# A gated pair of spectral filters: the order of every engine's work set by a list scheduler at build time

## The chip, the core and the metric

The kernel runs on one NeuronCore of a Trainium2 chip. Time is device time in microseconds (us) of one execution. The core has a matrix engine (PE), a vector engine (DVE), an activation engine (ACT), a general engine (POOL) and a sync engine (SP) that issues most DMAs. Each engine runs its own queue strictly in program order, and waits on semaphores that other engines or DMAs raise. An instruction that waits holds up everything behind it on its engine. PE writes only to PSUM, from where ACT or DVE copies ("evicts") to SBUF.

## The reference

x is one 2048 x 1024 matrix in bf16. Two branches filter it in the frequency domain with their own complex weights, and a gate per row mixes them:

```
g = sigmoid((A_x * gate_w).sum(-1, keepdims=True))          # one value per row
a = irfft2(rfft2(A_x) * (A_w_r + 1j * A_w_i))               # 2048 x 513 weights each
b = irfft2(rfft2(A_x) * (B_w_r + 1j * B_w_i))
out = g * a + (1 - g) * b
```

Both branches transform the same x, so the forward transform is computed once; B_x is not read.

## The kernel before, in words

The two-dimensional transforms are matmuls with constant cosine and sine matrices, in stages of 16 tiles each. Every tile is 128 partitions x 1024 f32 in PSUM. There are three PSUM slots for tiles, and one spare bank for small results (`m7`).

- **Fold** (`fold`, L365): DVE folds x along D by sums and differences, two tiles per step in four instructions.
- **S1** (in the loop at L385): PE, first part of the transform along S; ACT evicts to `Z`.
- **Gate**: `gate_w` is folded by DVE on one partition (four 1x512 instructions), PE turns it into columns (`G8`), four *gate rows* (`gate_row`, L379; eight 1x512 matmuls, each needs four `Z` tiles) give the gate's spectrum, sixteen small matmuls and one DVE product (`ZG`) give the *gated matrix's* input.
- **D** (`stage_d`, L421) needs all 16 `Z` tiles, gives `Q`; **S2** (`stage_s2`, L434) gives `X`, the spectrum.
- **Product** (`prod(b, m)`, L452): DVE multiplies two `X` tiles with the weights of branch b, eight steps per branch, two 2048-wide and two 1024-wide instructions each. `p512` does the same for the edge column.
- **I1** (`stage_i1(b, kg)`, L469): PE, inverse along S, gives `V` of branch b. A small DMA (`v512_row`, L514) adds row 0 once all 16 `V` tiles are out.
- **Inverse D** (`stage_dinv(b, n2)`, L518) needs all of `V` and row 0, gives `VA` or `VB`.
- **Gate broadcast** (`gmix`, L559): PE, a sigmoid on ACT, then two DVE instructions scale the last transform's matrix by g and 1 - g.
- **Last stage** (`s1inv`, L587): PE adds both gated branches in PSUM, ACT or DVE evicts, DVE *unfolds* in four instructions, SP stores 256 KB per tile.

Weights are loaded by `wload(b)` (L340) in 18 DMAs of 16 partitions on SP's queue, behind x and the constants. A product of branch b waits for the whole of its branch's weights (key `("W", b)`).

The order on every engine is the order in which the code records operations (`Sched.op`); `solve` then works out the semaphore waits. That order is written out by hand: loops over t interleave D of tile t, S2 of t - 1, I1 of t - 5 and a product on every second t (L537), then I1 of B with inverse D of A three tiles later (L571), then inverse D of B one tile ahead of the last stage (L611). Slots go round in turn. `ev` (L296) gives an eviction to ACT or DVE, whichever has less work summed up so far.

Of the kernel before, what the change touches and what calls it, by code (L numbers as in the profile page):

```python
# [4 lines left out]
dt = mybir.dt  # L5
# [111 lines left out]
class Op:  # L117
    __slots__ = ("eng", "idx", "fns", "deps", "raw", "dma", "clock", "need", "count", "waits", "pos")
# [8 lines left out]
class Sched:  # L127
# [9 lines left out]
    def op(self, eng, fns, reads=(), writes=(), dma=False):  # L137
        if not isinstance(fns, (list, tuple)):
            fns = [fns]
        o = Op(eng, len(self.q[eng]), list(fns), dma, len(self.all))  # L140
# [14 lines left out]
        o.deps.discard(o)  # L155
        return o
# [78 lines left out]
def bass_gated_mix__spectral_gfnet__spectral_gfnet__prompt_kernel(  # L235
# [45 lines left out]


    load = {"act": 0.0, "dve": 0.0}
    slot_n = [0]
    nslots = [3]

    def slot():
        s = slot_n[0] % nslots[0]
        slot_n[0] += 1
        return s  # L290

    def dve(ns, fns, reads, writes):
        load["dve"] += ns
        return S.op("dve", fns, reads, writes)

    def ev(n, outap, inap, reads, writes, eng=None, bias=0.0):  # L296
        ca, cd = 170 + 0.833 * n, 150 + 1.04 * n
        if eng is None:
            eng = "act" if load["act"] + ca <= load["dve"] + cd + bias else "dve"
        load[eng] += ca if eng == "act" else cd  # L300
        if eng == "act":
            S.op("act", lambda e: e.activation(outap, inap, ACT.Copy), reads, writes)  # L302
        else:
            S.op("dve", lambda e: e.tensor_copy(outap, inap), reads, writes)  # L304
# [4 lines left out]
    def misc(b, off, dims, np_=128):  # L309
        return ap(PS, b * 512 + off, dims, 0, np_)  # L310

    def mm(o, l, r, start, stop):
        return lambda e: e.matmul(o, l, r, start=start, stop=stop, skip_group_check=True)  # L313

    def tt(o, a, b, op):
        return lambda e: e.tensor_tensor(out=o, in0=a, in1=b, op=op)  # L316

    def dma(eng, pairs, reads, writes, kind=True):
        S.op(eng, [lambda e, d=d, s=s: e.dma_start(d, s) for d, s in pairs], reads, writes, dma=kind)  # L319

    def cload(eng, t, key, n):
        dma(eng, [(ap(t, 0, [[1, n]]).bitcast(dt.uint16), cst[key].ap())], [], [key])


    def xload(a, b):
        dma("sp", [(ap(R1, a * 1024, [[1024, b - a], [1, 1024]]), xv[:, a:b, :])], [], [("x", i) for i in range(a, b)])

    xload(0, 2)
    cload("sp", FM, "F", 2048)
    dma("act", [(ap(R2, 2048, [[1, 1024]], 0, 1), gate_w.rearrange("(o d) -> o d", o=1))], [], ["gw"])  # L330
    cload("act", ONE, "ONE", 2)
    for a, b in ((2, 4), (4, 8), (8, 12), (12, 16)):
        xload(a, b)
    cload("sp", DM, "DM", 2048)
    cload("sp", S2, "S2", 768)
    cload("sp", KI, "KI", 1024)
    cload("sp", GS, "GS", 16)
    cload("sp", ID, "ID", 16)

    def wload(b):  # L340
# [4 lines left out]
        for pm in range(2):  # L345
            for ii in range(4):
                for c in range(2):
                    src = wsrc[b][c]
                    n = src.shape[-1]

                    def part(r0, step, k0, k1):
                        prs.append((AP(T, (4 * pm + ii) * P + (2 * k0 + c) * NS, [[8 * P, 16], [2 * NS, k1 - k0], [1, n]]),
                                    AP(src.tensor, src.offset + r0 * n, [[128 * n, 16], [step * n, k1 - k0], [1, n]])))
                    if pm == 0:
                        part(16 * ii, 1, 0, 16)
                    elif ii < 3:
                        part(80 + 16 * ii, -1, 0, 16)
                    else:
                        part(127, -1, 1, 16)
                        part(64, 1, 0, 1)  # L360
        dma("sp", prs, [], [("W", b)] + (["zrow", "gwt"] if b else []))
    wload(0)


    def fold(n, src, soff, tmp, st, dst, doff, p0, np_, ns, reads, skey, writes):  # L365
# [5 lines left out]
        dve(ns, tt(Sx, lo, hi, ALU.add), reads, [skey + ("S",)])  # L371
        dve(ns, tt(Tx, lo, hi, ALU.subtract), reads, [skey + ("T",)])
        f = ap(tmp, st, [[1024, n], [512, 2], [1, 256]], p0, np_)
        r = ap(tmp, st + 511, [[1024, n], [512, 2], [-1, 256]], p0, np_)
        for i, op in enumerate((ALU.add, ALU.subtract)):
            o = ap(dst, doff + 512 * i, [[1024, n], [256, 2], [1, 256]], p0, np_)
            dve(ns, tt(o, f, r, op), [skey + ("S",), skey + ("T",)], [w + (i,) for w in writes])

    def gate_row(c):  # L379
        fns = [mm(misc(6, 0, [[1, 512]], 1), ap(G8, q, [[1, 1]]), ap(R3, q * 2048 + c * 32, [[128, 16], [1, 32]]), q == 0, q == 7)  # L380
               for q in range(8)]
        S.op("pe", fns, ["G8"] + [("Z", 4 * c + i) for i in range(4)], ["m6"])
        ev(512, ap(R2, c * 512, [[8, 16], [128, 4], [1, 8]], 0, 1), misc(6, 0, [[32, 16], [8, 4], [1, 8]], 1), ["m6"], [("zrow", c)])

    for n2 in range(0, 16, 2):  # L385
        st = n2 // 2 % 2
        fold(2, R1, n2 * 1024, RING, st * 2048, R4, n2 * 1024, 0, 128, 680,
             [("x", n2), ("x", n2 + 1)], ("st", st), [("u", n2), ("u", n2 + 1)])
        for m in (n2, n2 + 1):
            s = slot()  # L390
            fns = []
            for q in range(8):
                fns.append(mm(pslot(s, q * 128, [[1, 128]]), ap(R4, m * 1024 + q * 128, [[1, 128]]),
                              ap(FM, m * 128, [[1, 128]]), True, True))
            S.op("pe", fns, [("u", m, 0), ("u", m, 1), "F"], [("ps", s)])
            ev(1024, ap(R3, m * 8, [[128, 128], [1, 8]]), pslot(s, 0, [[8, 128], [1, 8]]), [("ps", s)], [("Z", m)],
               eng="act")
        if n2 == 2:
            fold(1, R2, 2048, R2, 4096, R2, 3072, 0, 1, 380, ["gw"], ("gst",), [("ug",)])
            fns = [mm(misc(7, q, [[1, 1]]), ap(R2, 3072 + q * 128, [[1, 128]], 0, 1), ap(ONE, 0, [[1, 1]], 0, 1), True, True)  # L400
                   for q in range(8)]
            S.op("pe", fns, [("ug", 0), ("ug", 1), "ONE"], ["m7", "gwt"])
            ev(8, ap(G8, 0, [[1, 8]]), misc(7, 0, [[1, 8]]), ["m7"], ["G8"], eng="act")
        if n2 % 4 == 2 and n2 > 2:
            gate_row(n2 // 4 - 1)
    gate_row(3)
    NZ = 16
    fns = []
    for n2 in range(16):
        w = ap(R2, n2 * 128, [[1, 128]], 0, 1)  # L410
        fns.append(mm(misc(7, n2, [[1, 1]]), w, ap(ONE, 0, [[1, 1]], 0, 1), True, True))
    S.op("pe", fns, [("zrow", c) for c in range(4)] + ["ONE"], ["m7", "zrow"])
# [233 lines left out]
```

## Time and profile before

| | us |
|---|---|
| median of 3 runs (161.98 to 162.6) | 162.08 |
| the profiled execution's own time | 160.53 |
| its span, first to last instruction | 159.0 |
| busy: PE / DVE / ACT / POOL | 124.6 / 120.4 / 121.7 / 0.2 |
| mean granted TensorE clock | 0.968 |
| DMA, all queues | 19.53 MB |

In the profile's rows all matmuls have one line (L313), all DVE arithmetic L316, all copies L302 (ACT) or L304 (DVE), since helpers record them; so they are told apart by tile names and shapes. `R` stands for the big buffers R1 to R5. A row of the timeline has start, length, engine, line, operation, output<-input, count, and in brackets the engine's idle time before it with what ended it. A row of issues has a DMA's count, size and the time from issue to landing. SPq is SP's queue.

### The profile page before, as it was taken

What the parts mean: (1) busy time and instruction counts of PE and PEld (TensorE: products, weight loads), DVE (VectorE), ACT (ScalarE), POOL (GpSimd) and SP (SyncE); (2) the same over time, 40 slices, a digit from 0 to 9 for tenths busy, and PEclk for the clock granted to TensorE, in tenths of its full rate; (3) what the DMA queues carried; (4) which work ended last, traced back from release to release, by engine and by line L of the source; (5) the groups of instructions that cost most, each with busy time, mean ns of one, the idle gap of its engine ahead of it and who ended that gap; (6) DMA issues with size and microseconds to landing.
All of it is one profiled execution on the core that took longest, in us unless ns stands there. A gap on an engine that the chain in (4) does not pass through costs nothing.

```text
span 159.0 us, 2541 instructions
## 1 busy us (share of the span) xinstructions
PE 124.6 (78%) x1015; PEld 90.0 (57%) x1024; DVE 120.4 (76%) x193; ACT 121.7 (77%) x132; POOL 0.2 (0%) x4
## 2 busy tenths in 40 slices
PE   0255897888928999999954999959999899898930
PEld 0244654355616767776633788847778576565600
DVE  0699998000079997998999999969923788989892
ACT  3045889629985988989955599999999499888850
POOL 0000000000000000000000000000000000000000
PEclk9999999999999999999995599999999999999995
DMA  5899999999999999950000000000000034243333
GB/s 168 296 429 415 257 168 167 177 167 165 179 168 170 181 169 169 197 191 4 0 0 0 0 5 0 0 0 4 0 0 1 4 112 152 86 180 123 145 132 132
DMA packets 13165, 19.53 MB, mean 123 GB/s; under 512 B 1505, under 2 KB 9825, under 8 KB 12770
## 3 DMA queue, kind: packets, MB, share of 16 engines
q1 hardware_dynamic: 13008, 19.37, 53.5%
q8 instruction: 8, 0.13, 0.4%
q14 instruction: 3, 0.02, 0.1%
q10 hardware_dynamic: 146, 0.00, 0.0%
HBM read 15.17 MB, written 4.19 MB: 122 GB/s over the span
## 4 chain that ended last, share of the span: by engine, by line
ACT 37%; PE 27%; DVE 22%; issue 7%; DMA 4%; SPq 1%; DVEq 0%
PE PS L313 27%; ACT R L302 21%; ACT RING L302 13%; DVE RING L316 12%; DVE R L316 6%; DMA R<-in_A_x_dram 4%; DVE RING L304 4%; ACT GROW L564 1%; ACT L564 1%; ACT V L302 1%; SPq L319 1%; DVEq L213 0%
## 5 line engine op out<-in xcount | busy, mean ns | idle before, releaser
L302 ACT ACTIVATE R<-PS 128x1024 bf16<-128x1024 f32 (+1 forms) x80 | 75.9, 1041 | 20.9 <-PE PS L313 20.9
L316 DVE TENSOR_TENSOR RING<-R 128x2048 bf16<-128x2048 bf16 (+1 forms) x48 | 48.0, 1041 | 16.9 <-DMA R<-in_A_w_i_dram 10.2
L302 ACT ACTIVATE RING<-PS 128x1024 bf16<-128x1024 f32 x40 | 42.8, 1135 | 8.0 <-PE PS L313 6.8
L316 DVE TENSOR_TENSOR RING<-RING 128x512 bf16<-128x512 bf16 (+1 forms) x96 | 44.6, 509 | 2.5 <-ACT RING L302 1.4
L313 PE MATMUL PS<-KI,RING 128*128 128x256 bf16 x256 | 34.0, 281 | 7.5 <-issue 3.1
L313 PE MATMUL PS<-DI,R 128*128 128x256 bf16 x256 | 32.7, 273 | 1.5 <-DVE RING L304 1.2
L313 PEld LDWEIGHTS PS<-KI,RING 128*128 128x128 bf16 x256 | 24.3, 101 | 14.0 <-issue 3.9
L313 PEld LDWEIGHTS PS<-DI,R 128*128 128x128 bf16 x256 | 24.4, 98 | 8.4 <-DVE RING L304 2.2
L313 PE MATMUL PS<-FM,R 128*128 128x128 bf16 x128 | 11.8, 266 | 13.0 <-DVE R L316 13.0
L313 PEld LDWEIGHTS PS<-FM,R 128*128 128x128 bf16 x128 | 10.1, 122 | 14.8 <-DVE R L316 14.4
L313 PE MATMUL PS<-RING,S 128*128 128x1 bf16 (+2 forms) x91 | 15.8, 304 | 1.3 <-ACT RING L302 1.1
L313 PE MATMUL PS<-DM,R 128*128 128x256 bf16 x128 | 16.4, 273 | 0.2 <-DVE RING L304 0.2
L313 PEld LDWEIGHTS PS<-DM,R 128*128 128x128 bf16 x128 | 12.0, 98 | 2.5 <-DVE RING L304 0.5
L313 PEld LDWEIGHTS PS<-RING,S 128*128 128x128 bf16 x96 | 7.8, 97 | 7.7 <-ACT RING L302 1.4
L304 DVE CAST RING<-PS 128x1024 bf16<-128x1024 f32 x8 | 10.0, 1251 | 1.9 <-PE PS L313 1.9
L316 DVE TENSOR_TENSOR R<-RING 128x1024 bf16<-128x1024 bf16 x16 | 10.3, 688 | 0.3
L313 PE MATMUL PS<-R,FM 128*128 128x512 bf16 x30 | 9.1, 379 | 1.3 <-DVE RING L304 1.3
L313 PE MATMUL PS<-RING,DM 128*128 128x512 bf16 x30 | 9.1, 379 | 0.1
L313 PE MATMUL PS<-R,G 128*1 128x512 bf16 x32 | 7.5, 378 | 0.7 <-ACT R L302 0.7
L304 DVE CAST R<-PS 128x1024 bf16<-128x1024 f32 x4 | 4.9, 1223 | 3.1 <-PE PS L313 3.1
L316 DVE TENSOR_TENSOR ZG<-PS,GS 128x16 bf16<-128x16 f32 x1 | 0.2, 175 | 6.8 <-PE PS L313 6.8
L313 PEld LDWEIGHTS PS<-RING,DM 128*128 128x128 bf16 x32 | 3.1, 98 | 3.8
(25 smaller groups left out, 26.9 us busy)
## 6 DMA issues: line engine op xcount, KB each, us to landing
out_dram<-RING SPq DMA_DIRECT2D x16, 256.0 KB, 2.0
R<-in_A_x_dram SPq DMA_DIRECT2D x3, 1024.0 KB, 10.5
R<-in_A_w_r_dram SPq DMA_DIRECT2D x7, 256.5 KB, 13.9
R<-in_A_w_i_dram SPq DMA_DIRECT2D x7, 256.5 KB, 14.7
R<-in_B_w_r_dram SPq DMA_DIRECT2D x7, 256.5 KB, 14.4
R<-in_B_w_i_dram SPq DMA_DIRECT2D x7, 256.5 KB, 14.1
R<-in_A_x_dram SPq DMA_DIRECT2D x2, 512.0 KB, 5.0
FM<-c_F SPq DMA_DIRECT2D x1, 512.0 KB, 5.0
```

The costliest lines, as they stand in the source:

```text
L302: S.op("act", lambda e: e.activation(outap, inap, ACT.Copy), reads, writes)
L304: S.op("dve", lambda e: e.tensor_copy(outap, inap), reads, writes)
L313: return lambda e: e.matmul(o, l, r, start=start, stop=stop, skip_group_check=True)
L316: return lambda e: e.tensor_tensor(out=o, in0=a, in1=b, op=op)
L319: S.op(eng, [lambda e, d=d, s=s: e.dma_start(d, s) for d, s in pairs], reads, writes, dma=kind)
L564: S.op("act", lambda e: e.activation(ap(GROW, 0, [[1, 512]]), misc(7, 0, [[1, 512]]), ACT.Sigmoid), ["m7"], ["GROW"])
```

## The change

Operations are no longer recorded in the order of the code. Each becomes a unit `U` with its engine, what it reads and writes, units that must come before it, a priority, and a rough duration. `run` takes streams of units (one list per stage, in order within the list). At each step it computes when the head of every stream could start, from `Sched.ready`, and records the one of highest priority among those within 40 ns of the earliest. So a fixed order comes out at build time, different on each engine. An eviction becomes a unit when its tile is recorded, and goes to the engine that would finish it first; it frees its PSUM slot, and a new tile takes any free slot. Besides:

- The fold of `gate_w` goes from DVE to POOL.
- The last gate row waits for the spectrum's edge column (`x5`), so it and what follows from it (gated matrix, `ZG`) come after S2. The gate's spectrum lies in `RM`'s first partition, so the load of `RM` now waits for it.
- Weights A are loaded in two halves (18 and 16 DMAs of half the rows), and a product waits only for its half. Weights B stay whole.
- The first product of B writes to a third buffer (`FM`, free by then) and needs no place among A's two.

```
+    def ready(self, eng, reads, writes):
+        t = self.free[eng]
+        for k in list(reads) + list(writes):
+            for d in self.writer.get(k, ()):
+                t = max(t, d.end + (60 if d.eng == eng else 160))
+        for k in writes:
+            for d in self.readers.get(k, ()):
+                t = max(t, d.end + (0 if d.eng == eng else 160))
+        return t
...
+            if self.eng == "ev":
+                n = self.n
+                ca, cd = 200 + 0.833 * n, 180 + 1.04 * n
+                ta, td = S.ready("act", self.reads, w), S.ready("dve", self.reads, w)
+                return (ta, "act", ca) if ta + ca <= td + cd + (300 if dnext[0] < td + 400 else 0) else (td, "dve", cd)
...
+            t0 = min(c[0][0] for c in cand)
+            r, u, s = min((c for c in cand if c[0][0] <= t0 + 40), key=lambda c: (c[1].prio, c[0][0]))
+            s.remove(u)
+            u.emit(r)
...
-        dma("sp", prs, [], [("W", b)] + (["zrow", "gwt"] if b else []))
-    wload(0)
+        return U(("ldw", b, ka), "sp", prs, [], [("W", b, k) for k in range(ka, kb)] + (["gwt"] if b else []),
+                 after, dma=(True, 1500.0 * (kb - ka)))
...
+             cload("sp", GS, "GS", 16), cload("sp", ID, "ID", 16), wload(0, 0, 8), wload(0, 8, 16),
+             wload(1, 0, 16, after=["G8mm"]), cload("sp", DI, "DI", 2048),
+             cload("sp", RM, "RM", 2048, ["zrow"], after=["gspec"])]
...
-            fold(1, R2, 2048, R2, 4096, R2, 3072, 0, 1, 380, ["gw"], ("gst",), [("ug",)])
+    gfold = [fold("gfold", 1, R2, 2048, R2, 4096, R2, 3072, 0, 1, ["gw"], ("gst",), [("ug",)], eng="pool", after=[("ld", "gw")])]
...
-    gate_row(3)
+        return U(("grow", c), "pe", ops, ["G8"] + [("Z", 4 * c + i) for i in range(4)], ["m7"], prio=6,
+                 after=["G8"] + [("evZ", 4 * c + i) for i in range(4)] + (["x5"] if c == 3 else []),
...
-        r = [("X", 2 * m), ("X", 2 * m + 1), ("W", b)]
+        rd = [("X", 2 * m), ("X", 2 * m + 1), ("W", b, 2 * m), ("W", b, 2 * m + 1)]
+        ok = (2,) if (b, m) == (1, 0) else (0, 1)
...
+        return U(("prod", b, m), "dve", ops, rd, after=[("evX", 2 * m), ("evX", 2 * m + 1), ("ldw", b, 0)], can=can, prio=2 + b)
...
-    for t in range(16 + 5):
-        if t < 16:
-            stage_d(t)
-        if 1 <= t < 17:
-            stage_s2(t - 1)
-        if t >= 5:
-            stage_i1(0, t - 5)
-        if t >= 2 and t % 2 == 0:
-            prod(t // 18, t // 2 - 1 - t // 18 * 8)
...
+    run([loads, aloads, folds, gfold, gate, [s1(n) for n in R16], [stage_d(k) for k in R16], [stage_s2(k) for k in R16],
+         [prod(0, m) for m in range(8)], [prod(1, m) for m in range(8)], [stage_i1(0, k) for k in R16],
+         [stage_i1(1, k) for k in R16], x5, [p512(0), p512(1)], [v512(0), v512(1)],
+         [stage_dinv(0, n) for n in R16] + [stage_dinv(1, n) for n in R16], [gmix(c) for c in range(4)],
+         [s1inv(n) for n in R16]])
```

Three places show what came of it. First PE, at the end of S1: `FM,R` are S1 tiles (eight matmuls each), `R,G` gate rows, `ONE,R` the gate's small matmuls, `DM,R` D tiles, `RING,S` S2. Before:

```order
L313 MATMUL PS<-FM,R 128x128 x32
L313 MATMUL PS<-R,G 1x512 x16
L313 MATMUL PS<-ONE,R 128x1 x16
L313 MATMUL PS<-DM,R 128x256 x16
L313 MATMUL PS<-RING,S 128x512 x2
```

Now:

```order
L314 MATMUL PS<-FM,R 128x128 x32
L314 MATMUL PS<-R,G 1x512 x8
L314 MATMUL PS<-FM,R 128x128 x16
L314 MATMUL PS<-DM,R 128x256 x24
L314 MATMUL PS<-RING,S 128x512 x2
```

Gate row 2 now stands ahead of the last two S1 tiles, gate row 3 and the gate's sixteen matmuls no longer stand ahead of D, and D and S2 go in threes.

Second DVE, around the edge columns (`P5`), where the products pass from A (weights in `R5`) to B (weights in `R2`); a product is the two rows with `128x2048` and `128x2x512`. Before:

```order
L316 TENSOR_TENSOR RING<-R4,R5 128x2048 x2
L316 TENSOR_TENSOR RING<-RING 128x2x512 x2
L316 TENSOR_TENSOR P5<-X5,R5 128x32 x2
L316 TENSOR_TENSOR P5<-P5 128x16 x2
L316 TENSOR_TENSOR P5<-X5,R2 128x32 x2
L316 TENSOR_TENSOR P5<-P5 128x16 x2
L316 TENSOR_TENSOR RING<-R4,R2 128x2048 x2
L316 TENSOR_TENSOR RING<-RING 128x2x512 x2
```

Now:

```order
L365 CAST R4<-PS 128x1024
L318 TENSOR_TENSOR RING<-R4,R2 128x2048 x2
L318 TENSOR_TENSOR FM<-RING 128x2x512 x2
L318 TENSOR_TENSOR RING<-R4,R5 128x2048 x2
L318 TENSOR_TENSOR RING<-RING 128x2x512 x2
L318 TENSOR_TENSOR P5<-X5,R5 128x32 x2
L318 TENSOR_TENSOR P5<-P5 128x16 x2
L318 TENSOR_TENSOR RING<-R4,R5 128x2048 x2
L318 TENSOR_TENSOR RING<-RING 128x2x512 x2
L318 TENSOR_TENSOR RING<-R4,R2 128x2048 x2
```

The first product of B (into `FM`) now stands ahead of the last two products of A; six products of A stand before it.

Third PE, from the last I1 tiles of B (`KI,RING`) to the last stage (`R3,FM` and `RING,DM`); `DI,R1` is inverse D of A, `DI,R5` of B, `RM,ZG` the gate broadcast:

```order
L314 MATMUL PS<-DI,R1 128x256 x24
L314 MATMUL PS<-KI,RING 128x256 x8
L314 MATMUL PS<-RM,ZG 128x128 x4
L314 MATMUL PS<-KI,RING 128x256 x8
L314 MATMUL PS<-DI,R1 128x256 x16
L314 MATMUL PS<-RM,ZG 128x128 x8
L314 MATMUL PS<-DI,R5 128x256 x24
L314 MATMUL PS<-R3,FM 128x512 x2
L314 MATMUL PS<-RING,DM 128x512 x2
```

Before, inverse D of B and the last stage alternated tile by tile, and three inverse-D tiles of A followed the last I1 tile; now inverse D of B comes in threes at first, and two tiles of A follow.

More of the change, by code (lines that the diff above doesn't have):

```diff
@@ L280, in bass_gated_mix__spectral_gfnet__spectral_gfnet__prompt_kernel @@
     WR = {0: R5, 1: R2}
[L283 to L304, printed above, removed]
+    VR = {0: R1, 1: R5}
@@ L331, in bass_gated_mix__spectral_gfnet__spectral_gfnet__prompt_kernel, with misc, mm @@
[L331 to L340, printed above, removed]
+    def misc(off, dims, np_=128):
+        return ap(PS, 7 * 512 + off, dims, 0, np_)
+    def mm(o, l, r, start=True, stop=True):
+        n = int(np.prod(o.shape[1:]))
+        return (lambda e: e.matmul(o, l, r, start=start, stop=stop, skip_group_check=True)), max(65.0, 0.42 * n)
```

448 lines of the change are left out of this document (270 added, 178 removed).

## The prediction

> **What bounds the kernel now.** I began with the page's busy line, then cut the span into stages at the events that end them: the last fold (27.43), the first D tile (34.09), the first product (44.59), the first product of branch B (83.28), the first inverse-D tile of B (122.0).
>
> ```profile
> span 159.0 us, 2541 instructions
> PE 124.6 (78%) x1015; PEld 90.0 (57%) x1024; DVE 120.4 (76%) x193; ACT 121.7 (77%) x132; POOL 0.2 (0%) x4
> ...
> 0.00:27.43 27.43, 14.51 (x136) 10.65 (x136) 21.57 (x36) 15.48 (x18) 0.20 (x4) 1.00 0.97 273
> 27.43:34.09 6.66, 5.25 (x48) 2.53 (x49) 0.00 (x0) 3.51 (x5) 0.00 (x0) 1.00 1.13 173
> 34.09:44.59 10.50, 9.40 (x76) 6.46 (x76) 0.18 (x2) 9.41 (x9) 0.00 (x0) 1.00 1.14 170
> 44.59:83.28 38.69, 33.00 (x267) 24.00 (x269) 36.38 (x46) 31.80 (x33) 0.00 (x0) 1.00 0.73 125
> 83.28:122.00 38.72, 34.20 (x308) 27.98 (x306) 31.97 (x42) 34.87 (x41) 0.00 (x0) 0.91 0.00 1
> 122.00:159.00 37.00, 28.23 (x190) 18.35 (x192) 30.28 (x70) 26.62 (x28) 0.00 (x0) 0.95 0.31 114
> ```
>
> The columns after the length are PE, weight loads, DVE, ACT and POOL busy, the granted clock, the DMA share and GB/s. No engine bounds the whole: three stand near 77%. But DVE does 0.18 us in the 17.16 us from 27.43 to 44.59. The waits and the timelines of DVE, PE and ACT say why.
>
> ```profile
> DVE RING L316 <- DMA R<-in_A_w_i_dram: 10.2, 1, 10.2
> DVE ZG L316 <- PE PS L313: 6.8, 1, 6.8
> ...
> 26.13 1.30 DVE L316 TENSOR_TENSOR R<-RING 128x1024 bf16<-128x1024 bf16 x2
> 44.59 2.36 DVE L316 TENSOR_TENSOR RING<-R 128x2048 bf16<-128x2048 bf16 x2 [10.21 <-DMA R<-in_A_w_i_dram]
> 46.87 1.29 DVE L316 TENSOR_TENSOR RING<-RING 128x1024 bf16<-128x1024 bf16 x2
> 48.07 2.35 DVE L316 TENSOR_TENSOR RING<-R 128x2048 bf16<-128x2048 bf16 x2
> 51.54 1.22 DVE L304 CAST R<-PS 128x1024 bf16<-128x1024 f32 x1
> ...
> 27.49 1.07 PE L313 MATMUL PS<-FM,R 128*128 128x128 bf16 x16 [1.19 <-DVE R L316]
> 28.48 1.89 PE L313 MATMUL PS<-R,G 128*1 128x512 bf16 x8
> 31.05 1.89 PE L313 MATMUL PS<-R,G 128*1 128x512 bf16 x8 [0.68 <-ACT R L302]
> 33.61 0.55 PE L313 MATMUL PS<-ONE,R 1*128 1x1 bf16 x16 [0.68 <-ACT R L302]
> 34.09 1.92 PE L313 MATMUL PS<-DM,R 128*128 128x256 bf16 x16
> ...
> 28.14 1.94 ACT L302 ACTIVATE R<-PS 128x1024 bf16<-128x1024 f32 x2 [0.31 <-PE PS L313]
> 39.73 1.02 ACT L302 ACTIVATE R<-PS 128x1024 bf16<-128x1024 f32 x1
> 90.94 12.94 ACT L302 ACTIVATE R<-PS 128x1024 bf16<-128x1024 f32 x14 [0.62 <-PE PS L313]
> ```
>
> Z15 is out at 28.14 + 1.94 = 30.08, yet D starts at 34.09: gate rows 2 and 3 and the gated matrix stand in PE's queue between them. X1 is out at 39.73 + 1.02 = 40.75, yet the first product starts at 44.59, when the last piece of weights A has landed. One product (two 2048-wide and two 1024-wide instructions) repeats after 48.07 − 44.59 = 3.48 us; a DVE cast costs 1.22; a plain ACT eviction 12.94 / 14 = 0.92; a PE tile about 0.9. The weights' own schedule is in the DMA rows:
>
> ```profile
> 18.00:44.00 26.00, 22.28 (x195) 13.56 (x194) 9.46 (x16) 20.64 (x23) 0.00 (x0) 1.00 1.14 170
> 44.00:68.00 24.00, 20.29 (x163) 14.84 (x167) 22.50 (x24) 19.65 (x21) 0.00 (x0) 1.00 1.13 177
> ...
> L319 SPq DMA_DIRECT2D R<-in_A_w_i_dram x9: 593/944/3659, 7.1 to 31.6; - x9
> L319 SPq DMA_DIRECT2D R<-in_B_w_i_dram x9: 592/1178/1455, 34.8 to 56.0; - x9
> ...
> R<-in_A_w_i_dram SPq DMA_DIRECT2D x1, 16.0 KB, 12.8
> R<-in_B_w_i_dram SPq DMA_DIRECT2D x1, 16.0 KB, 12.5
> R<-V SPq DMA_DIRECT2D x2, 4.0 KB, 1.7
> ```
>
> The DMA engines never rest from 18 to 68 at 170 to 177 GB/s. Weights A are complete at 31.6 + 12.8 = 44.4 and weights B at 56.0 + 12.5 = 68.5. The change moves neither byte nor place in that queue, so 68.5 is fixed, and I think it becomes the bound.
>
> **The change, part by part.** *Gate fold off DVE.* Four 1x512 instructions leave the fold chain:
>
> ```profile
> 10.71 1.53 DVE L316 TENSOR_TENSOR R<-R 1x512 bf16<-1x512 bf16 x4
> ...
> L319 SPq DMA_DIRECT2D R<-in_A_x_dram x5: 377/432/492, 0.7 to 3.1; - x5
> DMA to landing us min/median/max: 3.6/8.5/12.5
> ...
> L302 ACT ACT_TABLE_LOAD x1 | 1.3, 1283 | 1.7 <-PEq L631 1.7
> ```
>
> That takes 1.5 us off DVE, if x is there: the third of the five x loads, issued near 2.1, lands at the median 8.5 later, 10.6, as the third fold now wants it at 10.7. Folds end at 25.9. On POOL I have no such row; bounds are 1.5 us (as on DVE) and 4 x 1.3 + 1.3 = 6.5 us (each as long as the table load, and one such load besides). I take 4 us, nearer to 6.5, since POOL is new to it. PE's second gate step now waits for POOL before S1 tile 2, and PE is in order: if POOL ends after about 11, S1 slips until PE and ACT catch up, which they do by the last fold.
>
> The Trainium skill, "SBUF — State Buffer", § Who interferes with whom, states that a DVE instruction with two SBUF inputs and a GpSimd instruction that reads SBUF exclude each other for a whole instruction. By that rule the folds stand still while POOL runs, and the move gives the 1.5 us back and more; no row here has both engines busy. As a mechanism of this kernel it is priced among the rivals.
>
> *Gate row 3, gated matrix and gate product moved.* PE before D now holds gate row 2 (behind the S1 tiles of the last fold but one, 24.5 to 26.4), then S1 tiles 14 and 15 (1.07 us, to 27.5), and Z15 goes to DVE in 1.22: D starts at 28.7 instead of 34.09, 5.4 earlier. The moved steps cost PE the same 1.9 + 0.55 us later, in the wait for weights B below, so nothing; without that cover they cost 2.4.
>
> *Weights A in halves.* Half the bytes arrive half a transfer earlier: 44.4 less 2.1 MB / 170 GB/s = 12.4 gives 32.0. X1 is out about 6 us after D starts (before: 34.09 to 40.75, 6.7), at 34.7, so the first product starts at 34.8, 9.8 us earlier, waiting for X and not for weights. Sixteen more issues at the 0.6 us minimum of the rows above are at most 9.5 us of SP time, but SP runs some 12 us ahead of the landings: between 0 and that; I take 0.5.
>
> *The order of DVE.* Until weights B, DVE has six products of A and six casts: 6 x 3.48 + 6 x 1.22 = 28.2, and about 2 us of waiting for X tiles, so it arrives at product (B, 0) at 65.0. That instruction waits for all of weights B: 68.5 + 0.5 = **69.0**. Four us are lost there. Behind it in DVE's queue stand products (A, 6) and (A, 7), which are ready; behind them PE's inverse tiles 12 to 15 of A, the DMA of row 0, and all of branch B. So most of what the first 34 us win is spent waiting: earlier phases could slip by 4 us without moving the end.
>
> *From 69.0 to the first inverse-D tile of B.* DVE: ten products 34.8, edge products 2 x 0.6, gate product 0.2, two casts 2.4 and about 0.8 for a cast whose PE tile is late, which makes 108.4. Then tiles (B, 14), one gate broadcast and (B, 15) on PE, 2.3 with the eviction's latency; the last eviction is a DVE cast behind gm0, to 112.0; the DMA of row 1 takes 0.55 to issue and 1.7 to land, 114.2. ACT in the same stretch has 28 plain evictions (25.8), four sigmoids and a table load (3.3) and four small copies (1), 30.1 from about 81.5: 111.6, so it is as late as DVE and the two will get in each other's way through three PSUM slots; I add 1.0: **115.2**, against 122.0.
>
> *The last stage.*
>
> ```profile
> 123.06 1.23 DVE L304 CAST RING<-PS 128x1024 bf16<-128x1024 f32 x1 [0.61 <-PE PS L313]
> 126.68 3.14 DVE L316 TENSOR_TENSOR RING<-RING 128x512 bf16<-128x512 bf16 x8
> 151.76 4.49 DVE L316 TENSOR_TENSOR RING<-RING 128x512 bf16<-128x512 bf16 x12
> ```
>
> Before, 122.0 to the last unfold at 151.76 + 4.49 = 156.25: 34.25, of which DVE unfolds 16 tiles (3.14 / 2 less overlap, 1.48 each) with three casts between. Now PE runs it in threes, with four casts between unfolds: one more cast, 1.2, less the gaps it fills; I add 0.7: 34.95. Last unfold 150.15; the tail of 159.0 − 156.25 = 2.75 stays: span 152.9.
>
> The sum: 159.0 − 152.9 = 6.1 us. The profiled execution took 160.53 with a span of 159.0; the runs' median 162.08 is 1.55 above it. I subtract from the median: **156.0**.
>
> **The rivals.** *Less of it: a half clock and a blocked fold.* PE will wait from about 73 for product (A, 6) at 76. Before, after gaps near 80 to 83:
>
> ```profile
> 83.00:84.00 1.00, 0.88 (x10) 0.46 (x7) 1.00 (x5) 0.40 (x1) 0.00 (x0) 0.94 0.00 0
> 87.00:88.00 1.00, 0.99 (x12) 0.77 (x13) 1.00 (x2) 0.52 (x1) 0.00 (x0) 0.50 0.00 0
> ...
> 87.37 6.15 PE L313 MATMUL PS<-KI,RING 128*128 128x256 bf16 x40
> ```
>
> Five tiles took 6.15, 1.23 each instead of 0.9. Half clock for ten tiles costs up to 3.5 us of PE where DVE and ACT are also full; and folds that stand still for POOL's whole 6.5 us end at 32.4, which brings DVE to weights B at 71.5, 2.5 late. Either gives about 158.5. Against it: a gap of 3.1 us before 48.25 left the clock at 1.00. The Trainium skill, "TensorE: Matmul & The Clock Gate", § What's actually happening, puts the throttle after an idle window of about 3.4 us; by that rule this wait is on the edge, and the 0.50 rows agree with its half rate.
>
> *More of it.* If ACT, DVE and the slots mesh (no 0.8, no 1.0, no 0.7) and weights B land at 68.5: 3 us less, 153.0. It cannot be much less, since DVE's chain from weights B is counted without idle time.
>
> *No change.* Three slots and batches of three tiles may hold the middle stage at its old length, 122.0 − 34.09 = 87.9 us; from 28.7 that ends at 116.6, and with a last stage 5 us longer (each batch of three evictions draining before the next) the span is 116.6 + 42.0 = 158.6, the time 161.7. Against it: DVE's unfolds alone need 28 of the old 34.25.
>
> *Slower: SP cannot feed the halves.* The 18 issues of weights A began at 6.3 and the last at 31.6, 1.49 us apart. If that is SP's own work and not waiting for room in the queue, 34 half issues end at 6.3 + 50.6 = 56.9; the 18 of B, 1.3 apart (34.8 to 56.0 for 16 steps), end at 80, and weights B land 2 us behind: product (B, 0) at 82, 13 late, 169. It decides once a half issue takes over 1.29 us, since 6.3 + 43.9 + 23 + 2 = 75.2 is 6 us late. Against it: the shortest issue of full size took 0.59, and DMA has been busy throughout.
>
> **How the numbers follow.** Forecast 0.60 (154.5 to 157.5); less 0.17; more 0.12; no change 0.05; slower 0.06. A difference under 0.5% (0.8 us) is no change here. Faster 0.89, same 0.05, slower 0.06. The range takes in "more" and "less" with their own spread: 152.3 to 159.3.
>
> **What would show it right or wrong.** The first DM matmul near 29; the first product near 35; a DVE wait of 2 to 5 us on the B weights, ending at 69 ± 1; DVE nearly full until 108; the first inverse-D tile of B near 115; about 35 us from there to the last unfold. No wait on weights B, or one that ends after 72, makes the middle of the argument wrong; a D start after 33 makes the POOL step wrong; batches with DVE idle over 3 us in the last stage make that stage wrong.

## The result, and the profile after

The changed kernel takes 154.86 us (median of 4 runs, 153.14 to 155.68) against 162.03 before. The ratio is 0.949 (95% interval 0.939 to 0.959); like all ratios below it leaves out runs over 1.5% above a kernel's fastest, here two of the four, the profiled one among them. Timed once more beside the experiments it took 153.83 (153.41 to 155.82). The forecast was 156.0 with a range of 152.3 to 159.3: faster, by 7 to 8.5 us instead of 6. The profiled execution shown here took 155.47 us, with a span of 153.7; a second one, of 153.41 us and a span of 151.6, is shown behind it.

First the page's busy line and the windows of the changed kernel, cut at the same events as before (last fold, first D tile, first product, first product of B, first inverse-D tile of B):

```profile
span 153.7 us, 2554 instructions
PE 124.2 (81%) x1015; PEld 88.4 (58%) x1024; DVE 124.9 (81%) x193; ACT 118.7 (77%) x128; POOL 5.5 (4%) x8
...
0.00:26.46 26.46, 14.63 (x141) 10.17 (x142) 21.93 (x32) 15.50 (x18) 5.48 (x8) 1.00 0.96 278
26.46:29.75 3.29, 1.97 (x21) 1.10 (x20) 1.23 (x2) 1.89 (x3) 0.00 (x0) 1.00 1.14 167
29.75:35.72 5.97, 5.91 (x47) 4.21 (x49) 1.31 (x2) 4.46 (x5) 0.00 (x0) 1.00 1.15 172
35.72:68.73 33.01, 31.99 (x259) 23.48 (x260) 27.25 (x29) 31.68 (x31) 0.00 (x0) 1.00 1.12 175
68.73:116.53 47.80, 40.66 (x364) 31.62 (x366) 42.59 (x58) 38.52 (x46) 0.00 (x0) 0.96 0.04 12
116.53:153.70 37.17, 29.03 (x192) 17.85 (x192) 30.56 (x73) 26.70 (x28) 0.00 (x0) 0.97 0.31 114
```

The engines have as much to do as before, DVE even 4.5 us more (124.9 against 120.4, mainly since 16 evictions are DVE's instead of 12); what shrank is the time in which it had nothing to do. From the last fold to the first product 17.16 us have become 9.26.

Then the timeline's rows of POOL, DVE and PE at the steps that the prediction named (start, length, engine, line, operation, count, and in brackets the idle time and what ended it), and the rows of SP's issues of weights:

```profile
2.22 5.36 POOL L318 TENSOR_TENSOR R<-R 1x512 bf16<-1x512 bf16 x4 [1.78 <-DMA R<-in_gate_w_dram]
4.25 2.33 DVE L318 TENSOR_TENSOR RING<-R 128x1024 bf16<-128x1024 bf16 x2 [4.25 <-DMA R<-in_A_x_dram]
25.17 1.29 DVE L318 TENSOR_TENSOR R<-RING 128x1024 bf16<-128x1024 bf16 x2
25.55 1.89 PE L314 MATMUL PS<-R,G 128*1 128x512 bf16 x8
27.37 1.07 PE L314 MATMUL PS<-FM,R 128*128 128x128 bf16 x16
29.75 2.79 PE L314 MATMUL PS<-DM,R 128*128 128x256 bf16 x24 [1.32 <-DVE R L365]
35.72 2.36 DVE L318 TENSOR_TENSOR RING<-R 128x2048 bf16<-128x2048 bf16 x2 [2.70 <-ACT R L363]
68.73 2.36 DVE L318 TENSOR_TENSOR RING<-R 128x2048 bf16<-128x2048 bf16 x2 [3.40 <-DMA R<-in_B_w_i_dram]
76.04 1.34 PE L314 MATMUL PS<-KI,RING 128*128 128x256 bf16 x8 [2.87 <-DVE P L318]
109.07 1.29 DVE L318 TENSOR_TENSOR RING<-RING 128x1024 bf16<-128x1024 bf16 x2
112.94 1.22 DVE L365 CAST R<-PS 128x1024 bf16<-128x1024 f32 x1 [0.65 <-PE PS L314]
116.53 2.78 PE L314 MATMUL PS<-DI,R 128*128 128x256 bf16 x24
142.29 8.88 DVE L318 TENSOR_TENSOR RING<-RING 128x512 bf16<-128x512 bf16 x24
```

```profile
L358 SPq DMA_DIRECT2D R<-in_A_w_r_dram x17: 592/607/2105, 6.6 to 32.2; - x17
L358 SPq DMA_DIRECT2D R<-in_B_w_i_dram x9: 592/1058/1506, 34.2 to 56.0; - x9
```

D starts at 29.75 instead of 34.09, the first product at 35.72 instead of 44.59, and the bracket of that row now names ACT's X tile where before it named the weights. DVE arrives at product (B, 0) at 65.33 and waits 3.40 us for weights B, which land when they did before (68.73; the last issue still at 56.0). Behind it everything runs to the end.

The same rows of the second execution of the same kernel:

```profile
31.41 2.79 PE L314 MATMUL PS<-DM,R 128*128 128x256 bf16 x24 [1.32 <-DVE R L365]
68.37 2.36 DVE L318 TENSOR_TENSOR RING<-R 128x2048 bf16<-128x2048 bf16 x2 [1.39 <-DMA R<-in_B_w_i_dram]
107.00 1.29 DVE L318 TENSOR_TENSOR RING<-RING 128x1024 bf16<-128x1024 bf16 x2
110.87 1.22 DVE L365 CAST R<-PS 128x1024 bf16<-128x1024 f32 x1 [0.65 <-PE PS L314]
114.46 2.78 PE L314 MATMUL PS<-DI,R 128*128 128x256 bf16 x24
140.23 8.88 DVE L318 TENSOR_TENSOR RING<-RING 128x512 bf16<-128x512 bf16 x24
```

Here D starts 1.66 us later, DVE waits 2 us less for the weights, and yet the end comes 2 us earlier. The experiments below say why an earlier D can cost time.

### The profile page after: what moved, and what is told of

Its sections match the earlier page's. It is cut to its first block, busy times and chain, and to the rows that moved or that the text cites. A ratio compares the mean times of both kernels' runs of the same rounds, so it can differ in the third digit from the quotient of the medians.

```text
span 153.7 us, 2554 instructions
## 1 busy us (share of the span) xinstructions
PE 124.2 (81%) x1015; PEld 88.4 (58%) x1024; DVE 124.9 (81%) x193; ACT 118.7 (77%) x128; POOL 5.5 (4%) x8
## 4 chain that ended last, share of the span: by engine, by line
SPq 34%; PE 32%; ACT 10%; DVE 10%; DMA 8%; issue 4%; DVEq 0%
SPq L358 34%; PE PS L314 32%; DVE RING L318 9%; DMA R<-in_B_w_i_dram 8%; ACT R L363 6%; ACT RING L363 3%; DVE FM L318 1%; ACT L363 1%; ACT GROW L363 1%; DVEq L233 0%; DVE P L318 0%; DVE RING L365 0%; DVEq L219 0%
## 5 line engine op out<-in xcount | busy, mean ns | idle before, releaser
L363 ACT ACTIVATE R<-PS 128x1024 bf16<-128x1024 f32 x71 | 68.5, 1030 | 17.2 <-PE PS L314 17.0
L318 DVE TENSOR_TENSOR RING<-R 128x2048 bf16<-128x2048 bf16 (+1 forms) x48 | 49.0, 1062 | 10.7 <-DMA R<-in_A_x_dram 4.3
L318 DVE TENSOR_TENSOR RING<-RING 128x512 bf16<-128x512 bf16 (+1 forms) x94 | 42.6, 505 | 0.6
L314 PE MATMUL PS<-KI,RING 128*128 128x256 bf16 x240 | 30.4, 279 | 3.1 <-DVE P L318 2.9
L314 PE MATMUL PS<-DI,R 128*128 128x256 bf16 x256 | 30.9, 273 | 1.8 <-ACT R L363 1.8
L314 PEld LDWEIGHTS PS<-KI,RING 128*128 128x128 bf16 x240 | 22.8, 100 | 8.3 <-issue 3.6
L314 PE MATMUL PS<-DM,R 128*128 128x256 bf16 x128 | 15.0, 273 | 1.3 <-DVE R L365 1.3
L365 DVE CAST R<-PS 128x1024 bf16<-128x1024 f32 x9 | 11.0, 1223 | 5.9 <-PE PS L314 5.9
L365 DVE CAST RING<-PS 128x1024 bf16<-128x1024 f32 x7 | 8.7, 1249 | 6.0 <-PE PS L314 6.0
L314 PEld LDWEIGHTS PS<-R,FM 128*128 128x128 bf16 x32 | 2.6, 97 | 5.9 <-ACT RING L363 4.9
L318 POOL TENSOR_TENSOR R<-R 1x512 bf16<-1x512 bf16 x4 | 5.3, 1336 | 1.9 <-DMA R<-in_gate_w_dram 1.8
## 6 DMA issues: line engine op xcount, KB each, us to landing
R<-in_A_x_dram SPq DMA_DIRECT2D x3, 1024.0 KB, 10.7
```

Of the source, the lines that this page charges most:

```text
L314: return (lambda e: e.matmul(o, l, r, start=start, stop=stop, skip_group_check=True)), max(65.0, 0.42 * n)
L318: return (lambda e: e.tensor_tensor(out=o, in0=a, in1=b, op=op)), 150 + 0.523 * n
L363: S.op("act", lambda e: e.activation(o, i, f), self.reads, self.writes, ns=x)
L365: S.op("dve", lambda e: e.tensor_copy(o, i), self.reads, self.writes, ns=x)
```

## The experiments

Kernels called "frozen" replay the change's recorded order as a written-out list, so that only the edited piece differs; the scheduler does not plan again. Kernels were run in four groups, each with its own runs of the kernel before, whose medians were 162.32, 161.78, 162.91 and 162.5; so medians of different groups compare to about 1 us, and the ratios are the safer measure. The times of the marks are from each kernel's profiled execution.

| kernel | D starts | product (B, 0) | DVE's wait there | first inverse-D tile of B | span | median |
|---|---|---|---|---|---|---|
| before | 34.09 | 83.28 | none | 122.0 | 159.0 | 162.0 |
| the change, first execution | 29.75 | 68.73 | 3.40 | 116.53 | 153.7 | 154.86 |
| the change, again | 31.41 | 68.37 | 1.39 | 114.46 | 151.6 | 153.83 |
| weights B in halves | 32.04 | 67.53 | none | 114.29 | 151.5 | 153.02 |
| gate ahead of D | 34.36 | 69.84 | none | 115.23 | 152.4 | 153.66 |
| weights A whole | 31.51 | 75.58 | none | 122.41 | 159.9 | 161.69 |
| gate fold on DVE | 29.06 | 68.35 | 3.72 | 116.09 | 153.2 | 154.17 |
| gate fold on DVE, again | 30.63 | 68.59 | 2.41 | 114.89 | 152.0 | 153.81 |
| fold on DVE, gate row 3 twice | 29.27 | 68.49 | 3.66 | 114.64 | 151.8 | 154.01 |
| fold on DVE, weights B in halves | 30.94 | 66.42 | none | 113.34 | 150.5 | 151.37 |
| the same, planned anew | 32.17 | 54.59 | none | 116.45 | 154.7 | 156.61 |

**The change again.** The unedited kernel, as the mark for the next three.

> The changed kernel itself again, as the mark for the single edits beside it. Every theory: about 154 to 155.5 us, the wait of DVE on weights B again 3 to 4 us, and the idle share of PE around 73 to 76 with or without half clock behind it.

153.83, ratio 0.950 (0.941 to 0.959); its rows are above. The wait on weights B was 1.39 in the profiled execution, shorter than expected, because D started later.

**Weights A whole (frozen).**

```diff
-             wload(0, 0, 8), wload(0, 8, 16),
+             wload(0, 0, 16),
```

> The changed kernel's order, frozen, with one edit: weights A come whole, in 18 issues. My theory: the first product waits for them to about 44.5 instead of 35.7; DVE arrives at product (B, 0) about 5 us after weights B have landed, so the wait on weights B is gone and the time is about 5 us above the changed kernel's, 159 to 160. Rival (DVE only loses what it would otherwise wait for weights B, or makes it up): within 1 us of the changed kernel.

161.69, ratio to before 0.998 (0.994 to 1.002): 7.9 us above the change, and no faster than the kernel before. DVE and PE of this kernel:

```profile
44.88 1.23 DVE L398 TENSOR_TENSOR RING<-R 128x2048 bf16<-128x2048 bf16 x1 [10.10 <-DMA R<-in_A_w_i_dram]
48.54 3.57 PE L394 MATMUL PS<-KI,RING 128*128 128x256 bf16 x16 [6.70 <-issue]
75.58 2.35 DVE L398 TENSOR_TENSOR RING<-R 128x2048 bf16<-128x2048 bf16 x2
```

The first product comes at 44.88 as expected. I had expected 5 us and missed a part: PE stands in order behind the first I1 tiles for 6.70 us, and those tiles then take 3.57 where they take 1.92 in the change. Product (B, 0) is 7.2 us later than in the change's second execution and the first inverse-D tile of B 7.95 (122.41 − 114.46). The halves carry the gain: without them the scheduler's order, the moved gate and the fold on POOL together are worth nothing. (The order replayed here was planned for halves; a plan made for whole weights was not run.)

**Gate row 3 and the gated matrix ahead of D again (frozen).**

```diff
-                 after=["G8"] + [("evZ", 4 * c + i) for i in range(4)] + (["x5"] if c == 3 else []),
+                 after=["G8"] + [("evZ", 4 * c + i) for i in range(4)],
```

and in the list, gate row 3, its eviction, the gated matrix and ZG stand ahead of the first D tile.

> The changed kernel's order, frozen, with one edit: gate row 3, its eviction, the gated matrix and ZG stand ahead of D on PE again, as in the kernel before. My theory: D starts 2.4 to 4 us later, about 32 to 34, but DVE still arrives at product (B, 0) no later than weights B, because it had 3.4 us to spare there; the wait on weights B shrinks to near nothing and the time moves by less than 1 us. Rival (what the move wins at D passes through): 2 to 4 us slower than the changed kernel.

153.66 against 153.83: no difference. D starts 2.95 us later (34.36) and product (B, 0) 1.47 later:

```profile
34.36 2.79 PE L395 MATMUL PS<-DM,R 128*128 128x256 bf16 x24
69.84 2.35 DVE L399 TENSOR_TENSOR RING<-R 128x2048 bf16<-128x2048 bf16 x2
```

There is no wait in that row any more: the delay went into the slack ahead of weights B, and of what was left the first inverse-D tile shows 0.77. So moving the gate steps is worth nothing in the finished order, as long as weights B come whole.

**Weights B in halves too (frozen).**

```diff
-             wload(1, 0, 16, after=["G8mm"]),
+             wload(1, 0, 8, after=["G8mm"]), wload(1, 8, 16),
```

> The changed kernel's own order, frozen, with one edit: weights B also come in two halves, and product (B, m) waits for its half alone. My theory (the 3.4 us in which DVE waits for the whole of weights B is time on the path): the wait goes, everything behind it comes 3 us earlier, the first inverse-D tile of B at about 113.5 instead of 116.5, and the time is about 3 us below the changed kernel's. Rival (ACT, the slots and PE bound the stretch behind the wait anyway): product (B, 0) comes 3 us earlier, but the inverse-D tile of B at most 1 us, and the time by at most 1 us. Third way: the 16 more issues of SP hold up weights B themselves; then the last of it lands after 70 and the products of the second half wait.

153.02 against 153.83, 0.8 us less; the intervals of the ratios, 0.939 to 0.954 and 0.941 to 0.959, overlap, so this is not a clear difference. Product (B, 0) came 0.84 earlier, the first inverse-D tile 0.17. That fits neither theory well, because D started at 32.04 in this execution: there was little wait left to win. The sixteen more issues did not hold up weights B: no product waits for them. The same edit was therefore tried where D starts early, two experiments below.

**The gate fold on DVE, ahead of its first fold (frozen).** It was run in two groups.

```diff
-    gfold = [fold("gfold", ..., eng="pool", after=[("ld", "gw")])]
+    gfold = [fold("gfold", ..., eng="dve", after=[("ld", "gw")])]
```

> The changed kernel's order, frozen, with one edit: the gate fold runs on DVE ahead of its first fold instead of on POOL. Theory: the first two folds of x take 1.29 us per instruction again instead of 2.1 to 2.3, the folds end within 1 us of the changed kernel's, and the time moves by less than 1 us either way, since what is won or lost before D goes into the wait on weights B. Rival (POOL beside DVE costs DVE nothing but an x load that is late anyway): the folds end 1.5 us later, and that passes through.

> The change's frozen order with the gate fold on DVE, once more, as the mark for the two edits beside it: about 154 us, D near 29, DVE waiting 3 to 4 us on weights B until 68.4, PE idle about 3 us before the tiles of product (A, 6), and half clock in some 1 us stretches behind that.

154.17 and 153.81, beside 153.83 for the change: the same time. In the first execution the folds of x took 1.29 per pair again and ended at 25.84, 0.6 earlier than in the change, as the theory said. The two executions of this one kernel differ in an instructive way; the second is not as expected. The rows of gate row 0, the first D tiles, product (B, 0) and the first tile of product (A, 6), and the windows behind them; the first execution, then the second:

```profile
14.81 1.89 PE L394 MATMUL PS<-R,G 128*1 128x512 bf16 x8
29.06 2.79 PE L394 MATMUL PS<-DM,R 128*128 128x256 bf16 x24 [1.32 <-DVE R L445]
68.35 2.36 DVE L398 TENSOR_TENSOR RING<-R 128x2048 bf16<-128x2048 bf16 x2 [3.72 <-DMA R<-in_B_w_i_dram]
75.65 1.72 PE L394 MATMUL PS<-KI,RING 128*128 128x256 bf16 x8 [3.18 <-DVE P L398]
...
76.00:77.00 1.00, 1.00 (x7) 0.65 (x5) 1.00 (x1) 0.00 (x0) 0.00 (x0) 0.50 0.00 0
78.00:79.00 1.00, 1.00 (x6) 0.74 (x5) 1.00 (x3) 0.58 (x2) 0.00 (x0) 0.50 0.00 0
```

```profile
15.18 3.09 PE L394 MATMUL PS<-R,G 128*1 128x512 bf16 x8
30.63 2.79 PE L394 MATMUL PS<-DM,R 128*128 128x256 bf16 x24 [1.32 <-DVE R L445]
68.59 2.36 DVE L398 TENSOR_TENSOR RING<-R 128x2048 bf16<-128x2048 bf16 x2 [2.41 <-DMA R<-in_B_w_i_dram]
75.90 1.03 PE L394 MATMUL PS<-KI,RING 128*128 128x256 bf16 x8 [1.87 <-DVE P L398]
...
76.00:77.00 1.00, 1.00 (x11) 0.72 (x10) 1.00 (x4) 0.03 (x1) 0.00 (x0) 1.00 0.00 0
```

In the first, D starts 1.57 us earlier. Weights B come within 0.24 us of the same time, so PE runs out of work 1.3 us longer (3.18 against 1.87); behind that gap the granted clock (third column from the right) is 0.50 from 76 to 79, where the second shows 1.00. The first inverse-D tile of B is then 1.20 later (116.09 against 114.89), as is the end. The change's own two executions are the same pair: gap 2.87 and half clock in the one, 0.85 and full clock in the other. From product (B, 0) to the first inverse-D tile of B, the half clock costs 1.44 us in this pair (47.74 against 46.30) and 1.71 in the change's (47.80 against 46.09). Where it comes, an early arrival at weights B is thus not merely lost but turned into a loss.

**Gate row 3 twice, to fill that gap (frozen, fold on DVE).** The eight matmuls write the same sums again.

```diff
-               for q in range(8)]
+               for q in range(8)] * (2 if c == 3 else 1)
```

> The gate fold on DVE, weights B whole, and gate row 3's eight matmuls run twice (the same sums are written again), so that PE has 1.9 us more to do while DVE waits on weights B, and its gap there shrinks from 3.2 us to about 1.3. Theory (what costs an early D is the half clock that follows PE's gap): the clock stays at full rate from 68 to 85 and the time is 1 to 1.7 us below the run with the fold on DVE alone, though PE has more work. Rival (the clock's dip lies in time that DVE would take anyway): the same time within 0.5 us, or 1.9 us more.

The trace does what the theory says: with DVE's wait as long as in the first execution (3.66), the gap is 1.39, the clock is full from 68 to 85, and the first tile of (A, 6) takes 1.03:

```profile
68.49 2.36 DVE L398 TENSOR_TENSOR RING<-R 128x2048 bf16<-128x2048 bf16 x2 [3.66 <-DMA R<-in_B_w_i_dram]
75.80 1.03 PE L394 MATMUL PS<-KI,RING 128*128 128x256 bf16 x8 [1.39 <-DVE P L398]
```

From product (B, 0) to the first inverse-D tile of B it is 46.15 us, 1.59 less than in that execution, and the span, 151.8, is 1.4 below its 153.2. The median is not: 154.01 against 153.81 beside it. So the half clock is a loss of executions that fall into it, and filling the gap is no gain of the kernel that could be measured: the rival's "same time within 0.5 us" holds. The mean granted clocks suggest why. About 3 us at half clock in a span of 152 take 0.01 off the mean. With the fold on DVE the execution with half clock has 0.981; the other three of its group have 0.993 to 0.995, so they cannot have had as much. Of the second group the traced execution has none there, and two others have 0.991 and 0.994. So a median run probably has no half clock to lose; the other runs have no traces that would show it.

**Fold on DVE and weights B in halves (frozen).** The edits of the two above.

> The gate fold on DVE (so that D starts near 29 and DVE reaches product (B, 0) at about 64.6) and weights B in two halves as well. With weights B whole, product (B, 0) starts at 68.4. Theory (the wait on weights B is on the path): product (B, 0) at 64.6, the first inverse-D tile of B and the end 3 to 4 us earlier than in the run with the fold on DVE alone, about 150.5. Rival (ACT and the slots bound what comes behind): less than 1.5 us.

151.37 against 153.81, ratio to before 0.930 (0.922 to 0.938) against 0.947 (0.941 to 0.953): the fastest kernel of this study, 10.7 to 11.5 us below before.

```profile
30.94 2.79 PE L394 MATMUL PS<-DM,R 128*128 128x256 bf16 x24 [1.32 <-DVE R L445]
66.42 2.35 DVE L398 TENSOR_TENSOR RING<-R 128x2048 bf16<-128x2048 bf16 x2
113.34 2.78 PE L394 MATMUL PS<-DI,R 128*128 128x256 bf16 x24
```

Product (B, 0) starts without waiting, 2.17 earlier than in the run beside it, and the first inverse-D tile of B comes 1.55 earlier. The theory holds in kind, with two thirds passing through in this pair of executions; the 3 to 4 us expected assumed D at 29, and it started at 30.94. With the gate fold on POOL the same halves of weights B gave 153.02. So the fold's place, worth nothing while product (B, 0) waits for weights, is worth about 1.6 us once it does not: D starts at 30.94 against 32.04, the first inverse-D tile of B comes at 113.34 against 114.29. The intervals of the two ratios (0.922 to 0.938 and 0.939 to 0.954, different groups) only just miss each other, and D's start also differs between executions of one kernel, so this is likely rather than shown.

**The hand-written order of the kernel before, with one or both dependences changed.** First weights A in halves alone:

```diff
-    wload(0)
+    wload(0, 0, 8)
+    wload(0, 8, 16)
...
-        r = [("X", 2 * m), ("X", 2 * m + 1), ("W", b)]
+        r = [("X", 2 * m), ("X", 2 * m + 1), ("W", b, 2 * m), ("W", b, 2 * m + 1)]
```

> The kernel before, in its hand-written order, with one edit: weights A come in two halves and a product waits for its half. In the changed kernel's order the halves were worth 7.9 us (161.69 with weights A whole against 153.83). Theory: here the first product can start when X1 is out, about 40.8 instead of 44.6, so DVE gains 3.8 us and with its other work unchanged the time falls by about 3 us, to about 159. Rival (a hand-written order with turns of three slots cannot use the earlier weights): within 1 us of before, and the whole gain needs the scheduled order.

158.37, ratio 0.981 (0.972 to 0.989): 3.4 us, as expected. (Its profiled execution, with a span of 328.5 us, is unlike its other three of 157.87 to 158.49 and is not read; that the first product starts earlier is therefore not shown.) Then gate row 3 and the gated matrix alone, behind S2:

```diff
-    gate_row(3)
-    NZ = 16
...
         if t == 17:
             x512()
             p512(0)
             p512(1)
+            gate_row(3)
         if t == 19:
             v512(0)
             v512(1)
+            gspec()
```

> The kernel before, in its hand-written order, with one edit: gate row 3 and the gated matrix stand behind S2 (the gate's spectrum in the first partition of RM, RM loaded after that), and weights A whole. Theory: D starts near 30.3 instead of 34.1, but the products wait for weights A to 44.5 as before, and the time moves by less than 1 us. Rival: D's head start lets PE do more ahead of the products and 2 us or more are gained.

165.69, ratio 1.027 (1.019 to 1.035): 3.9 us **slower**, where I expected nothing.

```profile
45.80 2.36 DVE L316 TENSOR_TENSOR RING<-R 128x2048 bf16<-128x2048 bf16 x2 [18.54 <-DMA R<-in_A_w_i_dram]
...
91.82 0.17 DVE L316 TENSOR_TENSOR ZG<-PS,GS 128x16 bf16<-128x16 f32 x1 [1.83 <-PE PS L313]
...
49.47 1.86 PE L313 MATMUL PS<-KI,RING 128*128 128x256 bf16 x8 [8.27 <-issue]
82.93 1.89 PE L313 MATMUL PS<-R,G 128*1 128x512 bf16 x8 [1.20 <-ACT X L302]
```

D starts at 30.14, and all it wins is that PE idles 8.27 us instead of 3.10 ahead of the tiles of the first product, the first of which then runs at half clock (1.86 instead of 1.03). The gate steps had been free where they were, in the shadow of weights A. Behind S2 they stand in the way: 1.89 us on PE at 82.93, and DVE waits 1.83 for ZG in the midst of B's products. Besides, weights A landed 1.21 later in this execution (first product at 45.80 against 44.59); the rows do not say why, so the 3.9 us are not all traced. Both together:

> The kernel before, in its hand-written order, with both edits: weights A in halves, and gate row 3 with the gated matrix behind S2. Theory (the two dependences are the gain, the order only carries them): D near 30.3, first product near 37, seven us earlier than before, and the time near 154 to 156, as the changed kernel's. Rival (the scheduled order is a part of the gain of its own): 158 or more.

157.02, ratio 0.973 (0.964 to 0.982). With weights A in halves the move helps (158.37 to 157.02, with every run of the one above every run of the other), since D is then on the way to what the first product waits for: that product starts at 37.92, released by ACT. The time lies between what theory and rival expected, 3.2 us behind the change. A part of that is ZG again: DVE waits 1.80 us for it behind product (B, 0), against 1.11 and nothing in the change's two executions. The corners, and the price of the order:

| | weights A whole | weights A in halves |
|---|---|---|
| hand order, gate ahead of D | 162.0 | 158.37 |
| hand order, gate behind S2 | 165.69 | 157.02 |
| scheduler's order, gate behind S2 | 161.69 | 153.83 |
| scheduler's order, gate ahead of D | not run | 153.66 |

With the gate behind S2 the order recorded by the scheduler is worth 4.0 us in the one column and 3.2 in the other; with the gate ahead of D and weights A in halves it is worth 4.7 (158.37 to 153.66). These are differences across groups. (The scheduler's rows also have the gate fold on POOL, shown to be worth nothing with weights B whole, and the third product buffer, which no run takes away by itself.)

**The fastest edits, planned anew.** The scheduler makes the whole order itself, with the fold on DVE and weights B in halves; a product is also recorded only after the issue of its own half.

> The same two edits as the run with the fold on DVE and weights B in halves (151.4 us in the frozen order), but the scheduler plans the whole order anew with its own durations. Theory (the order is worth something where dependences change): the replanned order gains about 1 us more, near 150.5. Rival (the scheduler's rough durations and DMA times, not the edits, set how good its order is): the new order is no better than the frozen one, 151 to 154.

156.61, 5.2 us worse than the same edits in the frozen order (151.37).

```profile
28.66 3.57 PE L314 MATMUL PS<-R,G 128*1 128x512 bf16 x8 [0.26 <-DVE G L365]
32.17 3.15 PE L314 MATMUL PS<-DM,R 128*128 128x256 bf16 x24
116.45 2.79 PE L314 MATMUL PS<-DI,R 128*128 128x256 bf16 x24
```

It put the gate fold behind all folds of x, so a gate row with nothing to cover it stands just ahead of D, at half clock (3.57 instead of 1.89). The first inverse-D tile of B is 3.1 us later than in the frozen order. Of the 4.2 us by which the span is longer (154.7 against 150.5), D's start accounts for 1.2, the stretch from there to that tile for 1.9 and the last stage for 1.1; the last two were not taken apart. The scheduler does not know a good order from a bad one beyond its own rough durations; the order in the change happens to be good.

## Why the prediction was right, and where it was off

- **The gate fold.** Right in size: POOL took 5.36 us (taken: 4, bounds 1.5 to 6.5), folds ended at 26.46 (said: 25.9). The rule from the Trainium skill, "SBUF — State Buffer", § Who interferes with whom, that DVE with two SBUF inputs and a GpSimd instruction that reads SBUF shut each other out, agrees with the trace: DVE's first pair of fold instructions took 2.33 while POOL ran and 1.29 with the fold on DVE. But the folds did not stand still for POOL's whole time, as the prediction took that rule to mean: the first two pairs lost 1.04 and 0.83 us. It cost little because the second piece of x was late anyway (with the fold on DVE the second fold waits 0.32 for it); moving the fold back changed no time with weights B whole.
- **D at 28.7.** It was 29.75, and 29.06 to 32.04 over the frozen kernels with the gate behind S2. The step had PE and ACT catch up with the folds by the last one, and they did not: the last pair of S1 tiles (27.37) waits for no fold, since the last ended at 26.46; it stands behind gate row 2, which starts at 25.55 where 24.5 was said. S1 had begun at 8.79, against 7.00 before, and the step lacked PE's slow start, below; how much each adds was not separated. The gain from the gate's move was counted as a gain of D; the runs show that it is worth nothing in this order and −3.9 us alone.
- **First product at 34.8, waiting for X and not for weights.** 35.72, by ACT. This is the step that carries the result, and the experiment with weights A whole shows it. By itself, in the hand-written order, it is worth 3.4 us; the rest needs the order.
- **DVE at product (B, 0) at 65.0, released at 69.0.** 65.33 and 68.73. The 0.5 that I gave to sixteen more issues is not there: weights B landed at 68.73 and 68.37, where 68.5 was said without it. That the arrival fits to 0.3 us is partly luck: the first product was 0.9 late, and DVE did five casts on the way where six were counted. That the wait is time on the path is shown by weights B in halves with the fold on DVE: 2.4 us.
- **Products done at 108.4, last eviction of V at 112.0.** 110.36 and 114.16 in the first execution; 108.29 and 112.09 in the second, without half clock. The added slip of 1.0 before the first inverse-D tile is not there: from the last cast's start to that tile it is 3.59 us in both, where I had 4.4. DVE's time from product (B, 0) to the last one was 41.63 and 39.92, where I had 39.4.
- **Last stage 34.95.** From 116.53 to 142.29 + 8.88 = 151.17 it is 34.64, and 34.65 in the second execution. My sign against this step, DVE idle for over 3 us in the last stage, was badly set: DVE is idle for 4.1 us of it, as it was before (4.0 of 34.25), and the length came out all the same.
- **The step that was off** is the last: from a span of 152.9 to 156.0. I took the gain from the median, 1.55 above the profiled execution of before. The spans of the change, 153.7 and 151.6, lie on both sides of 152.9, but its medians are 154.86 and 153.83: the profiled execution is no fixed distance from the median, and here it was once above it. The second median, 153.83, lies below the band of 154.5 to 157.5 that I had given 0.60.

Of the rivals, "slower" is out: a half issue took SP 0.607 us in the median (it needed 1.29). "Less of it" has its mechanism, the half clock behind PE's wait, in the trace, but its price is 1.4 to 1.7 us in an execution that falls into it, not 2.5 to 3.5. "More of it", 153.0, needed no slip, which both executions show, and no longer last stage, which was 0.4 longer than the 34.25 of before; it is about as near to the medians as the forecast was. "No change" said that the stretch from D to the first inverse-D tile of B would keep its 87.9 us: it is 86.8 in the first execution (29.75 to 116.53) and 83.1 in the second, so that half of it was close where the half clock came in; it fails on the last stage, which did not grow.

## What to carry to other kernels

Ask of a step that stands in the way whether it stands in the shadow of a wait: the gate steps ahead of D were free as long as the weights were late, and moving them alone cost 3.9 us. Split the load whose last piece is waited for, and then look for the next load in the queue, since it takes over: here weights B, worth another 2.4 us where DVE reaches them early enough. A list scheduler's order is as good as its luck with rough durations; when its inputs change, measure the new plan against the old one, replayed.

## What the runs showed of the hardware

- Four 1x512 additions and subtractions took POOL 5.0 to 5.4 us (1.25 to 1.34 each), DVE 1.53 us for all four.
- PE starts slowly, and the granted clock does not show it: the first S1 tiles take 1.89 us per pair, later 1.07, with the clock at 1.00 in every window of that stretch. When the fast rate begins differs between executions of one kernel: gate row 0 took 1.89 in one and 3.09 in the other (rows above), and D started 1.57 apart. The Trainium skill, "TensorE: Matmul & The Clock Gate", § What's actually happening, has a free-running window for it, so that the moment varies; the trace agrees in kind, but the slow stretch lasts until about gate row 0, 6.5 us or more behind the first matmul, longer than the page's 3.4 us of sustained work. PE is not busy throughout (4.10 of the 6 us from 8 to 14 in the change), so this is no test of that figure.
- An idle gap of PE of 2.87 or 3.18 us was followed by half clock for 3 to 4 us; gaps of 1.87 and 1.39 were not, nor one of 3.10 in the kernel before. Nor is a single long gap needed: in the hand-written order with both edits no gap from 72 to 84 is over 1.20, but PE is busy only 0.82 and 1.18 us of the 2 from 80 to 82 and from 82 to 84, and the granted clock is 0.50 from 84 to 86. The same section's window of about 3.4 us that runs on its own would allow this scatter; no run here shows the window itself.
